# Second half of q and k of the first batch: from SP's queue with casts on chip to POOL's queue, cast on the way in

## The chip, the cores and the metric

The kernel runs on one core of one Trainium2 chip. The metric is the device time of one execution in microseconds (us), lower is better. Each kernel was executed several times; executions of two kernels are compared only where they ran in the same rounds on the same chip.

The profiles name the engines in short: PE is TensorE's matmuls (PEld its loading of weights), DVE is VectorE, ACT is ScalarE, POOL is GpSimd, SP is SyncE, which here only issues DMA transfers. "Clock" is the share of full speed that the profile shows as granted to TensorE.

## The reference

Symmetric sliding-window attention (8 batches, 8 heads, 576 positions, head size 64, window 32 to each side), then a two-layer network with an ELU over 4608 tokens:

```python
def _attn_ref(q, k, v):
    scores = scale * np.matmul(q, k.transpose(0, 1, 3, 2))
    mask = np.abs(pos[:, None] - pos[None, :]) <= 32
    scores = np.where(mask, scores, -1e9)
    attn = softmax(scores)                      # cut
    return np.matmul(attn, v)

def _moe_ref(x, w_in, w_out):                   # w_in 512x2048, w_out 2048x512
    h = x @ w_in
    g = np.where(h > 0.0, h, np.exp(np.minimum(h, 0.0)) - 1.0)
    return g @ w_out
```

Inputs and output are f32. The kernel computes in bf16 with f32 accumulation.

## The kernel before

Tokens go in 18 tiles of 256. A tile's hidden layer takes 8 steps (`mm1`), and so does its output layer (`mm2`); attention blocks are worked in pairs of 64 queries, two pairs to a tile. The first two tiles are interleaved: four hidden steps of the first, four of the second. A first step needs the pairs of its tile, so the start of the kernel is a race of loads: q and k (two halves of the first batch), values, and quarters of the weights.

```python
def load_qk(b, which, part, engs=(nc.sync, nc.sync)):       # f32 into SBUF, SP's queue
    ...
    for h in range(2):
        engs[h].dma_start(out=t[:, h, :], in_=src[:, :, h, :])

def load_v(b, m):                                           # f32 -> bf16 on the way, POOL's queue
    nc.gpsimd.dma_start(out=V_e[b % 3][p0:p1, m, :, 0:D], in_=...)

for which in range(2):
    load_qk(0, which, HALF_A, (nc.sync, nc.scalar))
...
for m in (1, 0, 2):
    load_v(0, m)
# ... masks ...
gate(masks[0:1, 3, 0:1])            # a 1-element DMA on SP: holds SP's queue until masks are done
for which in range(2):
    load_qk(0, which, HALF_B)       # four SP loads of 288 KB
load_w_in(0)                        # POOL's queue from here
for m in (3, 4):
    load_v(0, m)
load_w_out(0); load_w_in(1); load_w_out(1)
...
def transpose_qk(b, which, part, j0, n, evac, tag="t0"):
    for j in range(n):
        nc.tensor.transpose(pt[:, j * 128:(j + 1) * 128], src[:, j0 + j, :], ident)
    ...                              # eviction to qT or kT
...
# pairs 0 and 1, then hidden step 0 and 1, then:
front_cast(0, HALF_B, nc.scalar)     # f32 -> bf16 on ACT
front_cast(1, HALF_B, nc.vector)     # and on DVE
at(1, "mid", front_transpose, 1, HALF_B, nc.scalar, ("s", "u"))
at(1, "mid", front_transpose, 0, HALF_B, nc.vector, ("y0", "y1"))
for i, tag in ((2, "s"), (3, "u")):
    at(1, "mid", scores, i, tag)
    at(1, "mid", exponential, i)
    at(2, "dve", mask, i)
```

`idle(n, tag)` puts n matmuls on zeros into PE's program ("fillers"), to keep its clock up. `at(kk, slot, ...)` places work beside hidden step kk.

The softmax here doesn't subtract the row's maximum and nothing guards it: scores larger than these inputs give would overflow.

## Time and profile before

| | before |
|---|---|
| first three timed runs | 314.39, 320.15, 315.09 us |
| profiled run, its span | 310.77 us, 309.1 us |
| PE busy, of it in the first 30 us | 292.7 us, 22.3 us |
| second half of k landed | 17.4 us |
| hidden step 2 starts, first hidden step of tile 2 starts | 24.68, 27.98 us |

I call the last entry **the mark**. It is the first matmul of hidden step 4, and PE is nearly full from there on.

A line of VectorE's (DVE's) order of time, in the profile of the kernel before, shows the wait that the change is aimed at (start, length, instruction, then idle time before it and what ended it):

```profile
17.43 0.83 DVE L234 CAST qkb<-f 128x640 bf16<-128x640 f32 x2 [3.23 <-DMA f<-in_k_dram]
```

DVE sat idle for 3.23 us until k was there, and transposes, evictions and scores come behind it.

### The profile page before, as it was taken

What the parts mean: (1) busy time and instruction counts of PE and PEld (TensorE: products, weight loads), DVE (VectorE), ACT (ScalarE), POOL (GpSimd) and SP (SyncE); (2) the same over time, 40 slices, a digit from 0 to 9 for tenths busy, and PEclk for the clock granted to TensorE, in tenths of its full rate; (3) what the DMA queues carried; (4) which work ended last, traced back from release to release, by engine and by line L of the source; (5) the groups of instructions that cost most, each with busy time, mean ns of one, the idle gap of its engine ahead of it and who ended that gap; (6) DMA issues with size and microseconds to landing.
All of it is one profiled execution on the core that took longest, in us unless ns stands there. A gap on an engine that the chain in (4) does not pass through costs nothing.

```text
span 309.1 us, 7510 instructions
## 1 busy us (share of the span) xinstructions
PE 292.7 (95%) x2996; PEld 197.8 (64%) x3048; DVE 247.0 (80%) x480; ACT 170.6 (55%) x256; POOL 43.8 (14%) x60
## 2 busy tenths in 40 slices
PE   7768999999999999999999999999999999999994
PEld 3446666676666666666766666666666666666662
DVE  6677788899979788888888888888888787876663
ACT  3564756687664674667366736673636363634331
POOL 8733000834101112020202010000000000000000
PEclk9999999999999999999999999999999999999999
DMA  9999999999999999999989999488111111111011
GB/s 191 225 202 233 230 204 383 338 190 241 298 160 180 247 240 196 220 185 317 266 164 143 209 306 193 126 164 171 70 36 68 36 70 35 70 34 70 0 70 69
DMA packets 91657, 52.93 MB, mean 171 GB/s; under 512 B 76518, under 2 KB 80614, under 8 KB 91622
## 3 DMA queue, kind: packets, MB, share of 16 engines
q1 hardware_dynamic: 48022, 36.77, 46.7%
q0 software_dynamic: 41728, 8.92, 37.4%
q10 hardware_dynamic: 1872, 6.75, 6.7%
q8 instruction: 24, 0.39, 0.6%
q14 instruction: 11, 0.09, 0.1%
HBM read 36.70 MB, written 15.34 MB: 168 GB/s over the span
## 4 chain that ended last, share of the span: by engine, by line
PE 82%; DVE 7%; issue 3%; DMA 3%; ACT 2%; POOL 2%; SPq 1%; DVEq 0%; POOLq 0%
PE ps L558 38%; PE psY L592 36%; PE psS L320 3%; PE psS L288 3%; DMA f<-in_k_dram 3%; DVE g_sb L577 2%; DVE pm L308 1%; PE ptx L271 1%; DVE m_sb L567 1%; POOL Ve L129 1%; ACT e_sb L565 1%; DVE x_st L332 1%; ACT pu L299 1%; DVE y_sb L234 1%; SPq L123 1%
## 5 line engine op out<-in xcount | busy, mean ns | idle before, releaser
L565 ACT ACTIVATE e_sb<-ps 128x512 f32<-128x512 f32 (+1 forms) x145 | 86.2, 594 | 119.6 <-PE ps L558 112.8
L558 PE MATMUL ps<-xT,w_in_sb 128*128 128x256 bf16 x1152 | 149.3, 273 | 1.9 <-ACT xT L232 1.2
L592 PE MATMUL psY<-w_out_sb,g_sb 128*128 128x512 bf16 x525 | 139.1, 379 | 3.1 <-issue 0.6
L558 PEld LDWEIGHTS <-w_in_sb 128*128 128x128 bf16 x1152 | 110.7, 98 | 40.4 <-issue 2.2
L577 DVE SCALAR_TENSOR_TENSOR g_sb<-ps,m_sb 128x512 bf16<-128x512 f32 (+1 forms) x145 | 99.5, 686 | 12.9 <-PE ps L558 0.5
L567 DVE TENSOR_SCALAR m_sb<-e_sb 128x512 bf16<-128x512 f32 (+1 forms) x145 | 62.3, 430 | 33.0 <-ACT e_sb L565 30.8
L592 PEld LDWEIGHTS <-g_sb 128*128 128x128 bf16 x576 | 54.5, 98 | 38.3 <-DVE g_sb L577 0.2
L129 POOL DMA_DIRECT2D Ve<-in_v_dram x40 | 34.6, 876 | 131.7 <-PE psS L320 92.5
L299 ACT ACTIVATE pu<-psS 128x1024 bf16<-128x1024 f32 x36 | 36.5, 1020 | 3.5 <-PE psS L288 3.5
L232 ACT CAST qkb<-f 128x768 bf16<-128x768 f32 (+3 forms) x32 | 26.7, 838 | 0.0
L308 DVE TENSOR_TENSOR pm<-pu,masks 128x1024 bf16<-128x1024 bf16 x36 | 24.6, 683 | 1.9 <-ACT pu L299 1.8
L332 DVE TENSOR_TENSOR x_st<-psS,rc 128x512 bf16<-128x512 f32 x36 | 24.9, 692 | 1.2
L320 PEld LDWEIGHTS <-pm 128*64 128x64 bf16 x576 | 11.2, 110 | 10.5 <-DVE pm L308 7.4
L320 PE MATMUL psS<-Ve,pm 128*64 128x65 bf16 x320 | 13.7, 196 | 0.9 <-DVE pm L308 0.8
L140 DVE COPY Vo<-Ve 64x1040 bf16<-64x1040 bf16 x32 | 13.7, 428 | 1.0
L288 PE MATMUL psS<-qT,kT 64*128 64x64 bf16 x576 | 12.2, 193 | 2.4 <-DVE qT L234 1.9
L288 PEld LDWEIGHTS <-kT 64*128 64x128 bf16 x576 | 9.9, 96 | 7.0 <-issue 5.2
L234 DVE COPY y_sb<-psY 128x512 f32<-128x512 f32 x18 | 12.3, 686 | 1.1 <-PE psY L592 0.9
L320 PE MATMUL psS<-Vo,pm 128*64 128x65 bf16 x256 | 12.5, 197 | 0.2 <-DVE pm L308 0.2
L234 DVE CAST qkb<-f 128x1152 bf16<-128x1152 f32 (+3 forms) x14 | 9.2, 679 | 4.0 <-DMA f<-in_k_dram 3.6
L232 ACT COPY y_sb<-psY 128x512 f32<-128x512 f32 x18 | 10.5, 583 | 2.2 <-PE psY L592 2.2
L271 PE MATMUL ptx<-ident,qkb 128*128 128x128 bf16 x108 | 8.9, 235 | 1.7 <-DVE qkb L234 1.7
(32 smaller groups left out, 67.3 us busy)
## 6 DMA issues: line engine op xcount, KB each, us to landing
out_dram<-y_sb SPq DMA_DIRECT2D x35, 256.0 KB, 2.5
f<-in_q_dram SPq DMA_DIRECT2D x12, 576.0 KB, 9.0
f<-in_k_dram SPq DMA_DIRECT2D x12, 576.0 KB, 10.4
in_dram<-qkb ACTq DMA_DIRECT2D x10, 576.0 KB, 8.4
Ve<-in_v_dram POOLq DMA_DIRECT2D x24, 128.0 KB, 11.0
w_in_sb<-in_moe_w_in_dram POOLq DMA_DIRECT2D x4, 512.0 KB, 16.2
w_out_sb<-in_moe_w_out_dram POOLq DMA_DIRECT2D x4, 512.0 KB, 17.1
f<-in_q_dram SPq DMA_DIRECT2D x7, 288.0 KB, 6.3
```

What stands on the lines that cost most here:

```text
L129: nc.gpsimd.dma_start(out=V_e[b % 3][p0:p1, m, :, 0:D], in_=v[b, :, lo + p0:lo + p1, :].rearrange("h p d -> p h d"))
L232: nc.scalar.copy(d_, s_)
L288: nc.tensor.matmul(psS[:, h % 2, hp * 128 + z * QB:hp * 128 + (z + 1) * QB], lhsT=kT[b % 2][base:base + 64, KPAD + hp * S + QB * qb - WIN: ...
L299: nc.scalar.activation(pu, _bap(psS, [psS.ap[0], [1, 1024]]), AX.Exp, scale=SCALE)
L308: nc.vector.tensor_mul(pm, pu, _bap(mm, [mm.ap[0], [0, H], [1, 2 * QB]]))
L320: nc.tensor.matmul(psS[QB * z:QB * (z + 1), par, hp * VD:(hp + 1) * VD], lhsT=pm[:, par * HP + hp, z * QB:(z + 1) * QB], rhs=vv[:, qb // 2 ...
L332: nc.vector.tensor_mul(x_st, _bap(psS, [psS.ap[0], [VD, HP], [512, 2], [1, D]]), _bap(rc, [rc.ap[0], [2, HP], [1, 2], [0, D]]))
L558: nc.tensor.matmul(ps[:, j, :], lhsT=w_in_sb[:, do, fo * 128:(fo + 1) * 128], rhs=xT[t][:, :, do, :], start=(do == 0), stop=(do == NDO - 1))
L565: nc.scalar.activation(e_sb, ps, AX.Exp)
L567: nc.vector.tensor_scalar(m_sb, e_sb, -1.0, None, ALU.add)
L577: nc.vector.scalar_tensor_tensor(g_t[kk][:, z * w:(z + 1) * w, :], ps, 0.0, m_t[kk][z], ALU.max, ALU.min)
L592: nc.tensor.matmul(psY[t][ts], lhsT=g_sb[:, j, ts * 128:(ts + 1) * 128], rhs=w_out_sb[:, s * FG + j, :], start=(s == 0 and j == 0), stop=( ...
```

## The change

Its intent: get the second half of q and k out of SP's queue, where it competes with POOL's weights; put it in POOL's own queue at the place where it is wanted; let the DMA cast it; and so have it early enough to transpose between the first value products and score pairs 2 and 3 between hidden steps 0 and 1. Since a cast DMA lays the two heads of a couple out apart, each 128x128 transpose becomes a couple of 128x64 ones. Cut to its core:

```diff
+    def load_cast(b, which, part):
+        t = cpool.tile([128, 2, nj * D], BF16, name=f"c{which}")
+        ...
+        for h in range(2):
+            nc.gpsimd.dma_start(out=t[:, h, :], in_=src[:, :, h, :])
...
-    gate(masks[0:1, 3, 0:1])
-    for which in range(2):
-        load_qk(0, which, HALF_B)
-    load_w_in(0)
-    for m in (3, 4):
-        load_v(0, m)
-    load_w_out(0)
-    ...
+    for which in range(2):
+        load_cast(0, which, HALF_B)
+    load_w_in(0)
+    # two mask selects and a third
+    load_w_out(0)
+    for m in (3, 4):
+        load_v(0, m)
+    ...
+    gate(w_out_sb[0:1, NFO // 4 - 1, D_MODEL - 1:D_MODEL])   # was: w_in_at(1)
+    for which in range(2):
+        load_qk(1, which, HALF_A)
...
+                for h in range(2):
+                    nc.tensor.transpose(
+                        pt[64 * h:64 * (h + 1), j * 128:(j + 1) * 128],
+                        qk_c[b, which, z][:, h, (j0 + j) * D:(j0 + j + 1) * D], ident)
...
     pv(0)
-    idle(2, "h0")
+    front_transpose(0, HALF_B, nc.scalar, ("h0", "h1"))
     pv(1)
...
+    front_transpose(1, HALF_B, nc.vector, ("y0", "y1"))
     x_transpose(1)
-    front_cast(0, HALF_B, nc.scalar)
-    front_cast(1, HALF_B, nc.vector)
...
+    at(0, "mid", scores, 2, "s")
+    at(0, "mid", exponential, 2)
+    at(0, "mid", scores, 3, "u")
+    at(1, "mid", exponential, 3)
...
-            at(kq - 1 + which, "mid", cast_qk, 1, which, part, 0, SJ // 2,
+            at(*((kq + which, "dve") if kq == 7 else (kq - 1 + which, "mid")),
+               cast_qk, 1, which, part, 0, SJ // 2,
...
-        for n in {1: (0,), 2: (), 3: ()}.get(
+        for n in {1: (0,), 2: (), 3: (), 4: (), 5: (2,), 6: (3, 4)}.get(
```

More of the change, by code (lines that the diff above doesn't have):

```diff
@@ L123, in load_qk @@
             engs[h].dma_start(out=t[:, h, :], in_=src[:, :, h, :])
+    qk_c = {}
+    def load_cast(b, which, part):
+        z, nj = part
+        t = cpool.tile([128, 2, nj * D], BF16, name=f"c{which}")
+        qk_c[b, which, z] = t
+        src = (q, k)[which][b, :, z * NC * nj:(z + 1) * NC * nj, :].rearrange(
+            "(g h) (c j) d -> c g h (j d)", h=2, j=nj)
+        for h in range(2):
+            nc.gpsimd.dma_start(out=t[:, h, :], in_=src[:, :, h, :])
     def load_v(b, m):
@@ L183, in edges @@
                 nc.vector.memset(_bap(z, [z.ap[0], [S, n], [1, WIN]]), 0.0)
+    ident = cpool.tile([128, 128], BF16)
+    make_identity(nc, ident)
     edges(0)
     edges(1)
-    ident = cpool.tile([128, 128], BF16)
-    make_identity(nc, ident)
     masks = cpool.tile([128, 5, QB], BF16, name="masks")
@@ L202 @@
         load_v(0, m)
-    for mi in (0, 4):
-        nc.gpsimd.affine_select(
-            out=masks[:, mi, :], in_=masks[:, mi, :], compare_op=ALU.is_ge,
-            fill=0.0, base=-WIN, pattern=[[0, QB]], channel_multiplier=1)
-    nc.gpsimd.affine_select(
-        out=masks[:, 3, :], in_=masks[:, 3, :], compare_op=ALU.is_ge,
-        fill=0.0, base=128 - WIN - 1, pattern=[[0, QB]],
-        channel_multiplier=-1)
-    kinds = ["FE", "EE", "EL", "LF"]
-    gate(masks[0:1, 3, 0:1])
-    for which in range(2):
-        load_qk(0, which, HALF_B)
-    load_w_in(0)
-    for m in (3, 4):
-        load_v(0, m)
-    load_w_out(0)
-    load_w_in(1)
-    load_w_out(1)
+    kinds = ["FE", "EE", "EL", "LF"]
     def kind(jb):
@@ L264, in transpose_rows, with transpose_qk, evict @@
             out=keys_or_queries(b, which), in_=in_dram.pop((b, which)))
-    def transpose_qk(b, which, part, j0, n, evac, tag="t0"):
+    def transpose_qk(b, which, part, j0, n, evac, tag="t0", later=None):
         z, nj = part
-        src = qk_b[b, which, z]
         pt = ps_tile([128, 1024 if n <= 8 else 2048], BF16, tag, "ptx")
         for j in range(n):
-            nc.tensor.transpose(
-                pt[:, j * 128:(j + 1) * 128], src[:, j0 + j, :], ident)
-        d = keys_or_queries(b, which)
-        copy_on(evac,
-                _bap(d, [d.ap[0], [S, HP], [nj, NC], [1, n]],
-                     z * NC * nj + j0),
-                _bap(pt, [pt.ap[0], [1, HP], [HP, NC], [128, n]]))
+            if (b, which, z) in qk_c:
+                for h in range(2):
+                    nc.tensor.transpose(
+                        pt[64 * h:64 * (h + 1), j * 128:(j + 1) * 128],
+                        qk_c[b, which, z][:, h, (j0 + j) * D:
+                                          (j0 + j + 1) * D], ident)
+            else:
+                nc.tensor.transpose(
+                    pt[:, j * 128:(j + 1) * 128],
+                    qk_b[b, which, z][:, j0 + j, :], ident)
+        def evict():
+            d = keys_or_queries(b, which)
+            copy_on(evac,
+                    _bap(d, [d.ap[0], [S, HP], [nj, NC], [1, n]],
+                         z * NC * nj + j0),
+                    _bap(pt, [pt.ap[0], [1, HP], [HP, NC], [128, n]]))
+        if later is None:
+            evict()
+        else:
+            later.append(evict)
     st = {}
@@ L369, in front_cast, with front_transpose @@
             cast_qk(0, which, part, j0, n, eng)
-    def front_transpose(which, part, evac, tags):
+    def front_transpose(which, part, evac, tags, later=None):
         for (j0, n), tag in zip(SPLIT, tags):
-            transpose_qk(0, which, part, j0, n, evac, tag)
+            transpose_qk(0, which, part, j0, n, evac, tag, later)
     def idle(n, tag):
@@ L383 @@
     nc.scalar.activation(warm, zeros[:, 0:1], AX.Exp)
+    for which in range(2):
+        load_cast(0, which, HALF_B)
+    load_w_in(0)
+    for mi in (0, 4):
+        nc.gpsimd.affine_select(
+            out=masks[:, mi, :], in_=masks[:, mi, :], compare_op=ALU.is_ge,
+            fill=0.0, base=-WIN, pattern=[[0, QB]], channel_multiplier=1)
+    nc.gpsimd.affine_select(
+        out=masks[:, 3, :], in_=masks[:, 3, :], compare_op=ALU.is_ge,
+        fill=0.0, base=128 - WIN - 1, pattern=[[0, QB]],
+        channel_multiplier=-1)
+    load_w_out(0)
+    for m in (3, 4):
+        load_v(0, m)
+    for c in (1, 2):
+        load_w_in(c)
+        load_w_out(c)
+    for m in range(3):
+        load_v(1, m)
+    load_w_in(3)
+    load_w_out(3)
+    for m in range(3, VS):
+        load_v(1, m)
+    gate(w_out_sb[0:1, NFO // 4 - 1, D_MODEL - 1:D_MODEL])
+    for which in range(2):
+        load_qk(1, which, HALF_A)
+    gate(w_in_at(3))
+    for which in range(2):
+        load_qk(1, which, HALF_B)
+    for which in range(2):
+        load_qk(2, which, WHOLE)
     idle(8, "y1")
@@ L404 @@
         normalize(i)
-    for i in (0, 1):
-        idle(1, "h1")
-        x_transpose(i)
-        x_evac(i, nc.scalar)
-    idle(2, "h1")
-    front_cast(0, HALF_B, nc.scalar)
-    front_cast(1, HALF_B, nc.vector)
-    load_w_in(2)
-    load_w_out(2)
-    for m in range(3):
-        load_v(1, m)
-    load_w_in(3)
-    load_w_out(3)
-    for m in range(3, VS):
-        load_v(1, m)
-    gate(w_in_at(1))
-    for which in range(2):
-        load_qk(1, which, HALF_A)
-    gate(w_in_at(3))
-    for which in range(2):
-        load_qk(1, which, HALF_B)
-    for which in range(2):
-        load_qk(2, which, WHOLE)
+    x_transpose(0)
+    x_evac(0, nc.scalar)
+    front_transpose(1, HALF_B, nc.vector, ("y0", "y1"))
+    x_transpose(1)
+    x_evac(1, nc.scalar)
+    idle(2, "h1")
     tasks = {}
@@ L449, in pair_at @@
         at(kk + 2, "end", x_evac, i, nc.scalar)
-    at(1, "mid", front_transpose, 1, HALF_B, nc.scalar, ("s", "u"))
-    at(1, "mid", front_transpose, 0, HALF_B, nc.vector, ("y0", "y1"))
-    at(2, "dve", rotate_v, 0, 2, VS - 1)
-    for i, tag in ((2, "s"), (3, "u")):
-        at(1, "mid", scores, i, tag)
-        at(1, "mid", exponential, i)
-        at(2, "dve", mask, i)
-    at(2, "dve", lambda: mm2(1))
+    at(0, "mid", scores, 2, "s")
+    at(0, "mid", exponential, 2)
+    at(0, "mid", scores, 3, "u")
+    at(1, "mid", exponential, 3)
+    at(1, "dve", mask, 2)
+    at(2, "dve", lambda: mm2(1))
+    at(2, "dve", rotate_v, 0, 2, VS - 1)
+    at(2, "dve", mask, 3)
     for i in (2, 3):
@@ L472 @@
                nc.scalar, "s")
-    at(8, "dve", edges, 2)
+    at(6, "dve", edges, 2)
     at(16, "dve", hold_v, 2)
```

## The prediction

> **What bounds the kernel now.** I read the page first: the busy row, the slices, the chain. The span is 309.1 us (profiled run 310.77, median of the unprofiled runs 315.09).
>
> ```profile
> PE 292.7 (95%) x2996; PEld 197.8 (64%) x3048; DVE 247.0 (80%) x480; ACT 170.6 (55%) x256; POOL 43.8 (14%) x60
> ```
>
> TensorE is the bound, so only a stretch in which PE waits can give time. The table of busy times by stretch says where that is (columns: stretch, its length, busy us of PE, PEld, DVE, ACT, POOL, then granted clock, DMA share, GB/s).
>
> ```profile
> 10.00:15.00 5.00, 4.11 (x58) 1.92 (x52) 3.04 (x7) 2.69 (x4) 3.40 (x5) 1.00 1.20 275
> 15.00:20.00 5.00, 3.22 (x35) 2.56 (x34) 2.46 (x6) 3.95 (x7) 0.74 (x2) 1.00 1.52 209
> 20.00:25.00 5.00, 3.57 (x74) 2.19 (x75) 4.62 (x9) 1.94 (x2) 2.48 (x4) 1.00 1.24 206
> 25.00:30.00 5.00, 4.01 (x37) 3.23 (x37) 3.59 (x8) 2.74 (x5) 1.43 (x3) 1.00 1.22 228
> 30.00:35.00 5.00, 5.00 (x42) 3.44 (x41) 3.15 (x7) 2.90 (x5) 0.53 (x1) 1.00 1.58 266
> ```
>
> With the two earlier rows (3.59 and 3.76) PE is busy 22.26 of the first 30 us, and 20 of those matmuls are fillers on zeros. From 30 us on it is nearly full. So the change acts on a start-up of 30 us, and what it is worth is how much sooner PE reaches the full stretch. The mark I use is the first hidden-layer matmul of the second token tile, at 27.98. PE in order of time, around the hole:
>
> ```profile
> 15.32 1.91 PE L558 MATMUL ps<-xT,w_in_sb 128*128 128x256 bf16 x16 [0.24 <-ACT xT L232]
> 17.98 1.24 PE L271 MATMUL ptx<-ident,qkb 128*128 128x128 bf16 x18 [0.75 <-DVE qkb L234]
> 21.14 0.64 PE L288 MATMUL psS<-qT,kT 64*128 64x64 bf16 x32 [1.92 <-DVE qT L234]
> 21.80 1.90 PE L592 MATMUL psY<-w_out_sb,g_sb 128*128 128x512 bf16 x7
> 24.68 1.05 PE L558 MATMUL ps<-xT,w_in_sb 128*128 128x256 bf16 x8
> 27.98 1.03 PE L558 MATMUL ps<-xT,w_in_sb 128*128 128x256 bf16 x8 [0.94 <-ACT xT L232]
> ```
>
> And the chain of waits of the same stretch (start, length, what):
>
> ```profile
> 6.17 0.21 POOL masks L207
> 6.38 0.02 issue
> 6.39 0.75 SPq L151
> ...
> 9.29 8.12 DMA f<-in_k_dram
> 17.40 0.02 issue
> 17.43 0.83 DVE qkb L234 x2
> ...
> 19.73 1.36 DVE qT L234 x2
> 21.09 0.04 issue
> 21.14 0.42 PE psS L288 x16
> ```
>
> The second half of q and k sits behind a gate on the masks (6.39), is issued by SP from 7.20 to 9.9 and lands at 14.0 to 17.4. Then come casts (17.43), transposes (17.98), evictions to 21.09 and the scores of pairs 2 and 3. But the weights arrive hardly sooner. The list of DMA issues (KB, us to landing), for issues between 9.7 and 10.5 with the one before still running:
>
> ```profile
> w_out_sb<-in_moe_w_out_dram POOLq DMA_DIRECT2D x1, 512.0 KB, 12.9
> w_in_sb<-in_moe_w_in_dram POOLq DMA_DIRECT2D x1, 512.0 KB, 14.5
> ```
>
> The first quarter of w_out, issued at 8.88, lands at 21.8, and the first matmul on it starts at 21.80. The second quarter of w_in, issued at 9.80, lands at 24.3; its first use is at 24.68. So there are two bounds within half a microsecond: the q/k chain and POOL's queue. **Removing the q/k chain alone would gain next to nothing; the question is what the same bytes do to POOL's queue.**
>
> **What the Trainium skill says.** "DMA: Bandwidth & Descriptors", Rules for kernel authors, has casts during a DMA issued from GpSimd. The trace agrees: values and weights go from f32 in HBM into bf16 tiles that way, and queue 0 counts 8.92 MB over the run, half of the 17.8 MB of f32 read. The same page, Issuing engines are not separate DMA queues, says all issuers share the same 16 DMA engines. The trace agrees: from 12 to 14 us SP's queue took 0.58 MB and POOL's only 0.05 MB. "TensorE: Matmul & The Clock Gate", Part 3, says small matmuls on different column groups run at once. The trace agrees: 32 matmuls of the 128*64 form go in couples with the same start, 16 couples in 0.45 us, 28 ns a couple. Part 1 of that page puts the array at half rate after an idle window of about 3.4 us; here the first eight fillers take 0.45 us each and later ones about 0.21, and no later PE wait exceeds 1.92 us.
>
> **The change, part by part.**
>
> *Removed.* The gate and four SP loads of 288 KB; ACT casts at 15.16 (1.25 us), DVE casts at 17.43 (0.83); four fillers at about 0.21 us. All this lies in a stretch where PE waits, so only the end of the chain counts.
>
> *Added on POOL.* Four issues. Rows for w_in, w_out cost 0.76 to 0.94 each, so 4 x 0.76 = 3.0 us: 5.4 to 8.4 instead of nothing. w_in's first quarter is then issued at 8.4, not 6.33. The mask selects (1.0 us) end near 10.3; the first mask multiplication was at 10.97, so still in time.
>
> *Transfers.* In the trace POOL's queue moves 205 GB/s counted in bf16 on weights (0.82 MB from 20 to 24 us) and 153 on values (6 to 8 us). The first three values are through at 8.45. Behind them, with no other queue running:
> - q half, 2 x 147 KB: 1.44 us, to 9.9; k half, to 11.3.
> - w_in quarter 0, 524 KB: 2.56 us, to 13.85; w_out quarter 0: to 16.4.
> - two values, 246 KB at 153: 1.6 us, to 18.0; w_in quarter 1: to 20.6.
>
> A semaphore comes later than the bytes: adding up the moved bytes, w_out 0 was through at 19.7 and landed at 21.8, w_in 1 at 22.3 and 24.3; for the early values it was about 1.1. I choose 2.0 for all but values late in the queue (2.6). So q lands near 11.9, k 13.3, w_in 0 15.9, w_out 0 18.4, values 20.6, w_in 1 22.6. The new gate on w_out 0 lets the next batch's loads go near 19; at the old gates SP's bytes began 3 to 4.5 us after the issue, so w_in 1 is through before they compete.
>
> *PE up to the first hidden layer.* The first value product was at 11.7 to 12.1. The q transposes follow at once: 9 couples at about 55 ns, 0.5 us (the old 9 transposes took 0.50 to 0.58; a couple streams the same 128 columns). Second value product, transpose of x, then 0.5 us of k transposes near 13.6, second x transpose near 14.3, where it was 14.25. ACT's two evictions (0.75 + 0.62) fit after the exponentials end at 11.79 and before x at 13.85; DVE's k evictions (1.4 us) end near 15.7. The first hidden matmul then waits for w_in 0: **15.9, 0.6 later than the 15.32 of before.**
>
> *From there.* Hidden step 0 to 16.8; scores 2 and 3 (0.64) to 17.4; step 1 to 18.3. ACT takes 0.60 + 1.02 + 0.60 + 1.02 from 16.9; DVE 0.42 + 0.69 + 0.69 + 0.42 + 0.69, to about 20.4. Output step 0 starts at 18.5 (w_out there at 18.4), step 1 at 20.4. The values of 20.6 are rotated (0.88, to 21.5), the mask of pair 3 ends at 22.2, its value product at 22.65. Hidden step 2 starts then, w_in 1 being there at 22.6: 22.65 against 24.68. The same four steps as before follow (3.3 us), so the mark falls to 25.95 from 27.98. **Sum: +0.6 at the first hidden step, -2.6 behind it, 2.0 us gained.** The output steps put off to loop steps 5 and 6 keep w_out 1 (through near 26, landed near 27.5) off PE, with hidden step 5 in its place. After that PE is full and the 2 us go to the end undiminished.
>
> **Rivals.**
> 1. *POOL's queue stays the bound and gives nothing.* If cast rows of 2,304 B run at the 153 of the values, everything behind comes 1 us later; if the early SP loads take their share sooner, w_in 1 or w_out 1 is late by up to 3 us. For it: SP's 0.58 against 0.05 MB. Against it: total bytes per quarter do not grow, and the trough near 9 us (20 to 100 GB/s) goes. Time: 314 to 316.
> 2. *The landing lag is smaller without competition.* With the 1.1 of the early values the arrivals allow a gain of 3 us, but ACT and DVE then bind, through exponentials and masks. Time: 312 to 312.5.
> 3. *PE becomes the bound at the transposes or runs cold.* If couples do not overlap, 36 transposes add 1 us; with four fillers gone, a long wait for w_in 0 might halve the rate. Only transposes, products and two fillers remain from 12 to 15 us. Against: no gap over about 1 us is in sight. Time: 314 to 315.
> 4. *It is hidden anyway.* The casts' removal alone would be, by the w_out landing at 21.8. The reordering of w_out ahead of two values is what rescues it.
>
> **Range and chances.** 315.09 - 2.0 = 313.1. Rivals 1 and 3 pull to 315 or a little over, 2 to 312; fast runs differ by about 0.3%, 1 us, and an 0.8 us run spread is in the given times (314.39, 315.09). Range 310.9 to 315.4. Faster by over 2% needs 6.3 us, of the 7.7 idle in the first 30, which no step gives: 0.02. Slower by 6.3 us would take a hole of a kind that I do not see: 0.02.
>
> **What the after-profile shows if right.** The q half landing near 12 and k near 13.3; no q/k cast before the next batch; hidden steps 0 and 1 split by scores, at 15.5 to 16; step 2 near 22.6; the mark near 26; from 30 us the same full PE. Couples of transposes with the same start prove the 0.5 us. It is wrong if step 0 or 2 sits behind a weight landing later than I put it, if PE waits at the k transposes, or if PE, given the 2 us, loses them by 60 us through a wait for w_out 1 or for the next batch's casts.

## The result, and the profile after

The changed kernel took 309.59, 309.89, 310.10 and 309.13 us: **median 309.74**. The kernel before had a median of 314.74 us over four runs (the first three and one of 313.66 beside the changed kernel), or 314.39 over the three of them that are fast. The ratio is 0.985, interval 0.9816 to 0.9885; ratios here are the mean time of one kernel's fast runs over that of the other's in the same rounds, so not quite the ratio of the medians that I quote. Executions over 1.5% slower than the fastest of the same kernel are left out of the means. The predicted time was 313.1 and the range 310.9 to 315.4; the measured time lies below the range.

Later, both kernels ran on one chip in the same rounds: 313.02 against 309.73, ratio 0.9902 (0.986 to 0.9943). Later the kernel before was executed 44 times; the 43 fast ones took from 310.10 to 315.11, mean 312.85. Ten executions of the changed kernel have a mean of 309.87. So the gain is about **3 us, 1%**, and the first figure of 1.5% owes part of its size to the three earliest runs of the kernel before, whose median of 315.09 no later call reached. They were not traced, so what they lost is open.

PE in order of time in the changed kernel's profile, the lines that answer to the six of before (`ptx<-ident,c` are the couples of transposes; L582 is the hidden layer, L296 scores, L616 the output layer):

```profile
11.83 0.67 PE L266 MATMUL ptx<-ident,c 128*64 128x128 bf16 x18
13.57 0.69 PE L266 MATMUL ptx<-ident,c 128*64 128x128 bf16 x18
15.27 1.03 PE L582 MATMUL ps<-xT,w_in_sb 128*128 128x256 bf16 x8 [0.46 <-ACT xT L226]
16.23 0.64 PE L296 MATMUL psS<-qT,kT 64*128 64x64 bf16 x32
18.72 1.02 PE L616 MATMUL psY<-w_out_sb,g_sb 128*128 128x512 bf16 x3 [0.87 <-DMA w_out_sb<-in_moe_w_out_dram]
22.64 1.05 PE L582 MATMUL ps<-xT,w_in_sb 128*128 128x256 bf16 x8 [0.36 <-DMA w_in_sb<-in_moe_w_in_dram]
25.95 1.91 PE L582 MATMUL ps<-xT,w_in_sb 128*128 128x256 bf16 x16 [0.94 <-DVE m_sb L591]
```

Both transposes run without a wait, scores 2 and 3 start at 16.23 and not at 21.14, and the wait for q and k is gone. Hidden step 2 starts at 22.64 (before 24.68) and waits 0.36 us for w_in's second quarter. The mark is at 25.95, which is the very figure that I had predicted (to the hundredth by chance: in a second profile of the same kernel it is 26.09). POOL's part, in order of time:

```profile
5.38 1.12 POOL L135 DMA_DIRECT2D c<-in_q_dram  x2
6.46 1.32 POOL L135 DMA_DIRECT2D c<-in_k_dram  x2
7.75 0.78 POOL L167 DMA_DIRECT2D w_in_sb<-in_moe_w_in_dram  x1
```

The four issues take 2.4 us, and the first quarter of w_in goes out at 7.75 instead of 6.33. The chain of waits of this profile now has one long piece in the start-up:

```profile
11.50 11.10 DMA w_in_sb<-in_moe_w_in_dram
22.59 0.05 issue
22.64 1.06 PE ps L582 x8
```

That is POOL's queue delivering the second quarter of w_in: this queue now bounds the start-up, though only by the 0.36 us that PE waits for it at 22.64.

So the trace of the changed kernel came out as told, and still the time was missed by 3.4 us. Comparing the two profiles gives 310.77 - 309.59 = 1.2 us: 2.0 at the mark, of which 0.8 is lost behind it. The rest of the answer is in the kernel before: its first profile was of one of its quickest executions. The experiments are about that.

### The profile page after: what moved, and what is told of

Read it like the earlier page. It is cut to its first block, busy times and chain, and to the rows that moved or that the text cites. A ratio compares the mean times of both kernels' runs of the same rounds, so it can differ in the third digit from the quotient of the medians.

```text
span 307.9 us, 7525 instructions
## 1 busy us (share of the span) xinstructions
PE 291.5 (95%) x3009; PEld 196.9 (64%) x3062; DVE 245.8 (80%) x478; ACT 169.4 (55%) x254; POOL 45.8 (15%) x64
## 4 chain that ended last, share of the span: by engine, by line
PE 81%; DVE 7%; DMA 4%; POOL 3%; issue 2%; ACT 1%; DVEq 0%; POOLq 0%
PE ps L582 38%; PE psY L616 36%; DMA w_in_sb<-in_moe_w_in_dram 4%; PE psS L328 3%; PE psS L296 3%; DVE g_sb L601 2%; POOL Ve L141 1%; PE ptx L271 1%; DVE m_sb L591 1%; DVE x_st L340 1%; DVE pm L316 1%; ACT e_sb L589 1%; POOL c L135 1%; DVE y_sb L228 1%; PE psXT L349 1%
## 5 line engine op out<-in xcount | busy, mean ns | idle before, releaser
L582 PE MATMUL ps<-xT,w_in_sb 128*128 128x256 bf16 x1152 | 149.3, 273 | 2.7 <-DVE m_sb L591 0.9
L616 PE MATMUL psY<-w_out_sb,g_sb 128*128 128x512 bf16 x525 | 139.1, 379 | 4.2 <-DMA w_out_sb<-in_moe_w_out_dram 0.9
L582 PEld LDWEIGHTS <-w_in_sb 128*128 128x128 bf16 x1152 | 110.7, 98 | 41.0 <-issue 2.3
L616 PEld LDWEIGHTS <-g_sb 128*128 128x128 bf16 x576 | 54.5, 98 | 39.9 <-DVE g_sb L601 1.6
L226 ACT CAST qkb<-f 128x768 bf16<-128x768 f32 (+1 forms) x30 | 25.4, 848 | 0.0
L296 PEld LDWEIGHTS <-kT 64*128 64x128 bf16 x576 | 10.0, 97 | 5.3 <-issue 4.2
L296 PE MATMUL psS<-qT,kT 64*128 64x64 bf16 x576 | 12.4, 193 | 0.5 <-DVE kT L228 0.5
L226 ACT COPY qT<-ptx 128x1152 bf16<-128x1152 bf16 (+2 forms) x8 | 7.5, 971 | 3.1 <-PE ptx L271 2.4
L271 PE MATMUL ptx<-ident,qkb 128*128 128x128 bf16 x90 | 7.1, 223 | 2.0 <-DVE qkb L228 1.9
```

What stands on the lines that cost most here:

```text
L226: nc.scalar.copy(d_, s_)
L296: nc.tensor.matmul(psS[:, h % 2, hp * 128 + z * QB:hp * 128 + (z + 1) * QB], lhsT=kT[b % 2][base:base + 64, KPAD + hp * S + QB * qb - WIN: ...
L582: nc.tensor.matmul(ps[:, j, :], lhsT=w_in_sb[:, do, fo * 128:(fo + 1) * 128], rhs=xT[t][:, :, do, :], start=(do == 0), stop=(do == NDO - 1))
L616: nc.tensor.matmul(psY[t][ts], lhsT=g_sb[:, j, ts * 128:(ts + 1) * 128], rhs=w_out_sb[:, s * FG + j, :], start=(s == 0 and j == 0), stop=( ...
```

## The experiments

The theories at the start: **A**, in the kernel before, the SP loads and POOL's loads compete, and k lands sometimes much later than in the first profile; **B**, the array clock falls back in the hole behind the wait for k; **C**, only another chip. Behind all of them stands the prediction's account of the changed kernel, part by part.

### The kernel before again: e0_before_again, h1_before_look, h2_before_look, h3_before_look

No edit. Four more executions were profiled.

> The kernel before, unchanged. Its profiled run took 310.77 us, its timed runs 313.66 to 320.15, while the changed kernel took 309.13 to 310.10 everywhere. Theory A (the old start-up has a wait that comes and goes, because the SP loads of q and k and POOL's loads of weights compete for the 16 DMA engines): times spread over 3 us or more, from about 310.5 to 315, and if the profile falls in a long run it shows a weight or q/k landing later than in the first profile by the amount lost. Theory B (the array clock is granted late or falls back in some runs of the old kernel): the long runs list a granted clock below that of the short ones, with the landings where they were. Theory C (nothing but another chip): all runs of the kernel before on this chip lie within 1 us of each other and the ratio of this copy to it is 1.000.

> The kernel before, one more profile. Theory A (landing of k): a run of 312.5 to 315 has k landing at 18.5 to 20.5, its mark (first hidden step of the second tile) moved by the same, and 282.5 to 283.5 us behind the mark. Theory B (clock): k near 17.5, a clock of 0.5 to 0.6 for some 3 us before the mark. Neither: mark near 28 and more than 284 us behind it.

> As the one before it, another execution: the same three readings. If theory A holds in both, mark minus k landing stays at 10.6 to 11.7 without a clock fall-back, and is about 1.4 more with one.

> As the two before it, a third execution. Over the three: if the times differ by over 1 us, the landings of k should differ by about the same (theory A), or the clock should have fallen back in the longer ones alone (theory B).

The copy e0 took 311.94 (310.11 to 313.16) beside 312.54 (311.07 to 315.11), ratio 0.9966 (0.9927 to 1.0004). So C is out as it stood: on one chip, one kernel spreads over 4 us, and its copy differs by 0.3% with five rounds. DVE's line for the cast that waits for k, in e0, then in h1:

```profile
17.74 0.83 DVE L234 CAST qkb<-f 128x640 bf16<-128x640 f32 x2 [4.03 <-DMA f<-in_k_dram]
```

```profile
18.63 0.83 DVE L234 CAST qkb<-f 128x640 bf16<-128x640 f32 x2 [4.57 <-DMA f<-in_k_dram]
```

k came 0.3 us later in e0 and 1.2 later in h1. And busy times by stretch (its length, then PE, PEld, DVE, ACT, POOL, then the granted clock, DMA share, GB/s), first the first profile of before, then e0:

```profile
18.00:20.00 2.00, 1.21 (x18) 1.07 (x19) 1.89 (x5) 1.37 (x2) 0.56 (x1) 1.00 1.31 205
20.00:22.00 2.00, 0.84 (x33) 0.63 (x33) 1.97 (x4) 0.42 (x1) 1.19 (x2) 1.00 1.24 205
22.00:24.00 2.00, 1.95 (x23) 0.92 (x22) 1.68 (x4) 1.52 (x2) 0.84 (x1) 1.00 1.24 206
24.00:26.00 2.00, 1.78 (x36) 1.55 (x31) 1.86 (x5) 0.24 (x1) 0.74 (x1) 1.00 1.24 206
```

```profile
18.00:20.00 2.00, 1.24 (x18) 1.01 (x18) 1.89 (x6) 1.22 (x2) 1.31 (x2) 1.00 1.24 205
20.00:22.00 2.00, 0.55 (x32) 0.61 (x32) 1.97 (x4) 0.24 (x2) 1.27 (x2) 1.00 1.25 207
22.00:24.00 2.00, 2.00 (x13) 0.77 (x7) 1.67 (x4) 1.84 (x2) 0.34 (x1) 0.58 1.24 206
24.00:26.00 2.00, 2.00 (x36) 0.89 (x34) 0.58 (x2) 0.00 (x0) 0.40 (x1) 0.57 1.24 207
```

In the column of the clock, e0 has 0.58 and 0.57 from 22 to 26 us, where the first profile has 1.00. The instructions show it too: output steps 0 and 1, with the value products of pair 2 or 3 not counted, stretch over 3.35 us from 22.03, against 1.90 from 21.80. All five profiles of the kernel before, unchanged:

| profile | cast of k starts | clock under 0.9 near 20 to 26 us | scores of pair 2 start | step 2 | mark | mark minus cast | mark minus scores | time | time minus mark |
|---|---|---|---|---|---|---|---|---|---|
| first | 17.43 | no | 21.14 | 24.68 | 27.98 | 10.55 | 6.84 | 310.77 | 282.8 |
| e0 | 17.74 | yes | 21.45 | 26.11 | 29.41 | 11.67 | 7.96 | 312.38 | 283.0 |
| h1 | 18.63 | yes | 22.70 | 27.38 | 30.69 | 12.06 | 7.99 | 313.68 | 283.0 |
| h2 | 17.95 | yes | 21.66 | 25.99 | 29.30 | 11.35 | 7.64 | 311.90 | 282.6 |
| h3 | 18.14 | yes | 21.84 | 26.18 | 29.48 | 11.34 | 7.64 | 312.05 | 282.6 |

The last column hardly moves, so all the difference between these executions arises ahead of the mark. **Both A and B hold.** The first profile is the one with the earliest k and the only one without a fall-back. The mean cast start is 17.98, so 0.55 later than in the first profile. From the cast to the scores all take 3.70 or 3.71 us except h1, which takes 4.07, as one DVE instruction there (L567) takes 0.79 us and not 0.42. From the scores to the mark the four with a fall-back take 0.80 to 1.15 us more than the first profile, 0.97 on average, 0.77 spread over five. Together with h1's 0.36 (0.07 over five) that is 1.39, and the mean mark of 29.37 is 1.39 behind the first one. (How the DMA engines share is told in "DMA: Bandwidth & Descriptors", Queues, rings and completion order: each engine goes round the queues that have work, packet by packet. The order of arrival here fits such sharing; which packet held up which is not shown for these five.)

In the hole, PE was not wholly idle. From the start of hidden step 0 to the scores, h2 (15.81 to 21.66) and the first profile (15.32 to 21.14) have the same pattern: 3.16 and 3.15 us busy, with waits of 0.77 and 1.92 in the one, 0.75 and 1.92 in the other. Yet h2's clock fell, at 21.1, and the first profile's did not. "TensorE: Matmul & The Clock Gate", Part 1, has the activity window run free, of about 3.4 us; equal business with different outcome agrees with that, and so does the length of the fall-backs: each of the four lasts 3.4 us, in h2 from 21.1 to 24.5.

The executions that were not traced list a mean clock, and it goes with the time. Of the 43 fast ones, the eight with 0.997 or more took 310.10 to 311.62, mean 310.94; the other 35 took 311.07 to 315.11, mean 313.29. This does not say where in a run the clock fell, and not every fall costs time: h3 has another one from 7.6 to 11 us, and its hidden step 0 still starts at 15.21.

### Fillers in the hole: f1_before_fillers

```diff
+    at(1, "mid", idle, 4, "y0")
     at(1, "mid", front_transpose, 1, HALF_B, nc.scalar, ("s", "u"))
     at(1, "mid", front_transpose, 0, HALF_B, nc.vector, ("y0", "y1"))
+    at(1, "mid", idle, 5, "h0")
```

> The kernel before with nine more filler matmuls in the two idle stretches between hidden step 1 and the scores of pair 2 (17.0 to 18.0 and 19.2 to 21.1 in its profile), nothing else. In the second profile of the kernel before, the granted clock was 0.58 and 0.57 from 22 to 26 us, after PE had been busy 2.67 of the 6 us from 16 to 22, and hidden step 2 started at 26.11 instead of 24.68; in the first profile it stayed at 1.00 after 3.30 of 6 busy. Theory B (the array clock falls back behind this hole in most executions): no fall-back here, times near 310.5 to 311 and hardly spread, 1 to 2 us below the kernel before. Theory A (competition of transfers): the fillers change nothing, 312 to 313, spread as before.

It took 312.48 (310.79 to 313.22) beside 313.64 (310.10 to 314.33 without the slow one), ratio 0.9962 (0.9914 to 1.0009): a gain of 1.2 us in the medians that the interval does not secure. In the profile the clock stayed at 1.00 throughout the first 30 us, and all six executions list 0.997 or more, where ten of the eleven beside them list 0.995 or less. So fillers do keep the clock up. PE at the scores and at the mark:

```profile
23.18 0.64 PE L288 MATMUL psS<-qT,kT 64*128 64x64 bf16 x32 [0.91 <-DVE qT L234]
30.04 1.03 PE L560 MATMUL ps<-xT,w_in_sb 128*128 128x256 bf16 x8 [0.94 <-DVE m_sb L569]
```

Between the two lie 6.86 us, as in the first profile (6.84) and within 0.01 of e3, g1, f5 and h4, which have no fall there either, and unlike the four with a fall-back (7.64 to 7.99): the extra time there is the clock's. But k landed late, its cast at 19.02. Of the 2.06 us by which this mark is behind the first profile's, 1.59 is the late k and 0.45 lies between cast and scores, where again one DVE instruction was long (0.88 us). B by itself does not make the kernel as quick as its first profile, nor as the changed kernel. The expected 310.5 to 311 was a miss.

### The first quarter of w_out ahead of two values: e3_before_wout_first, f4_wout_first_fillers

```diff
     load_w_in(0)
+    load_w_out(0)
     for m in (3, 4):
         load_v(0, m)
-    load_w_out(0)
```

f4 has the fillers of f1 as well.

> The kernel before with only the first quarter of w_out put ahead of the last two values on POOL's queue. My prediction said that this reordering rescues the change; in the kernel before the q and k chain ends at 21.1 us in any case, so alone it should give at most 0.5 us if the profile of before is typical. If timed runs of before are long because w_out's first quarter lands late (theory A), it takes 2 to 4 us off, to 310.5 to 312. If theory B or C holds, it stays within 0.5 us of the kernel before.

> The earlier run with the first quarter of w_out ahead of the last two values (315.43, against 312.54 of the kernel before) with the same nine fillers. Theory B: that run was long because the clock fell back twice, so with the fillers it comes to 311 to 312.5. Theory A (its two values land later and hold the value products up): it stays at 314 to 315.5.

e3 took 315.43, ratio 1.0082 (1.0044 to 1.012): slower by less than 2%, but clear of the noise, where I had expected nothing or a gain. f4 took 313.89, ratio 1.0019 (0.9974 to 1.0065). In the profiles k's cast started at 18.86 (e3, the quickest of its six runs at 312.75) and at 20.83 (f4, 315.58). DVE's line in f4:

```profile
20.83 1.20 DVE L234 CAST qkb<-f 128x640 bf16<-128x640 f32 x2 [6.63 <-DMA f<-in_k_dram]
```

DVE waited 6.63 us for k, and PE's clock was at 0.50 from 20.4 to 27.3 us, in and behind so large a hole, nine fillers or not. So moving POOL's loads about, with SP's loads untouched, changes when SP's loads land: that is the competition of theory A, and the way in which the kernel before was exposed to it. The counts of packets show it. From 14 to 16 us, SP's queue moved 257 packets with 0.51 MB in the first profile, and POOL's 628 small ones of values with 0.08 MB. With w_out's larger packets in the place of the values, it was 187 packets with 0.38 MB against 191 with 0.19 MB in f4, and 189 with 0.40 MB against 189 with 0.19 MB in e3. From 16 to 18 us SP's queue had 0.02 MB left to move in the first profile, 0.29 in f4 and 0.40 in e3. (e3's profile lost more than that: its first half of k was late as well, with its cast at 8.56 where before had 6.44, the clock was at 0.50 from 9.0 to 15.8, and hidden step 0 started at 18.28. That load was issued before anything which e3 changed, so this part is chance.)

### SP's loads without the gate: g1_no_gate

```diff
-    gate(masks[0:1, 3, 0:1])
     for which in range(2):
         load_qk(0, which, HALF_B)
```

> The kernel before without the gate on the masks: the four SP loads of q and k's second half go out at 2.1 us instead of 7.2, ahead of POOL's values and weights. In five profiles of the kernel before and its variants the last of them landed at 17.4, 17.7, 18.9, 19.0 and 20.8 us, and the time of the run followed: 310.77, 312.38, 312.75, 312.59, 315.58. If this landing is what makes the kernel before long and uneven (theory A): it lands by 12 us, the casts no longer wait, the rest is bound by w_in's second quarter (24.3 before), and the time is 310 to 311.5 with a spread under 1.5 us, though the first value products start 1 to 2 us later. If the clock is the cause (theory B), or what is left after these is the same, 312 to 314.

It took 313.29 (312.67 to 314.63), ratio 1.001 (0.997 to 1.0051): no gain. k no longer keeps anything waiting (its casts start at 16.95, in turn and with no wait), but DVE's and PE's lines show what came in its place:

```profile
12.68 0.43 DVE L140 COPY Vo<-Ve 64x1040 bf16<-64x1040 bf16 x1 [2.24 <-DMA Ve<-in_v_dram]
```

```profile
18.16 1.91 PE L557 MATMUL ps<-xT,w_in_sb 128*128 128x256 bf16 x16 [0.24 <-ACT xT L231]
```

The values are late now: their copy starts at 12.68 where before had 9.08, hidden step 0 at 18.16 instead of 15.32, and the mark at 29.68. The first half of k was late too (its cast at 7.82, before 6.44). Early or late, the same bytes of q and k in a second queue cost the first pairs or the second ones. I had expected 310 to 311.5 from the landing of k alone; its place relative to the values counts as much. With the two starts tried for SP's loads (behind the masks, and at once) it did not come between the first three values and the weights; in POOL's queue the program puts it just there. A gate on the values themselves, with SP's queue kept, was not tried.

### The transport alone, and its place in the queue: f5_loads_only, h4_loads_behind_w_in

f5 is the changed kernel with PE's order of before: transposes after hidden step 1, then scores 2 and 3, and the four fillers back.

```diff
     pv(0)
-    front_transpose(0, HALF_B, nc.scalar, ("h0", "h1"))
+    idle(2, "h0")
     pv(1)
...
-    front_transpose(1, HALF_B, nc.vector, ("y0", "y1"))
...
-    at(0, "mid", scores, 2, "s")
...
+    at(1, "mid", front_transpose, 1, HALF_B, nc.scalar, ("s", "u"))
+    at(1, "mid", front_transpose, 0, HALF_B, nc.vector, ("y0", "y1"))
+    for i, tag in ((2, "s"), (3, "u")):
+        at(1, "mid", scores, i, tag)
```

h4 is f5 with the cast loads behind the first quarter of w_in:

```diff
+    load_w_in(0)
     for which in range(2):
         load_cast(0, which, HALF_B)
-    load_w_in(0)
```

> The transport part of the change alone: cast loads of q and k on POOL's queue, no casts on chip, couples, new gate and output places, but PE's order of before, the transposes after hidden step 1 and scores 2 and 3 behind them. If the landings set the gain (my prediction's account: w_in's second quarter at 22.6), hidden step 2 starts at 22.6 to 23.2 and the time is within 0.5 us of the changed kernel, 309.5 to 310.5. If the order is what fills the hole and keeps the clock up (theory B), PE idles some 2 us while the evictions run near 19, and part of the executions are 1.5 us longer: median 310.5 to 312.

> The earlier run with the transport part alone (310.61), with the four cast loads of q and k behind the first quarter of w_in instead of ahead of it, still in POOL's queue. If one queue instead of two is what counts: q and k land near 15 to 16.5 in every execution, hidden step 0 starts at 15.0 to 15.5 instead of 16.2, and the time is 309.8 to 310.8 with a spread under 1.5 us. If the place ahead of the weights counts: the landings come after hidden step 1 is done, PE waits for them, 311.5 to 313.

f5 took 310.61 (310.13 to 311.21), ratio 0.9915 (0.9873 to 0.9958), so the transport brings most of the gain or all of it; its new queue and the removal of the casts on chip come together in it and were not tried apart. Its profile has the mark at 27.74, 1.8 behind that of the changed kernel; one piece of that is hidden step 0, at 16.20 behind a 0.91 us wait for w_in, and there is no fall-back. h4 took 310.73 (309.58 to 312.06), ratio 0.9964 (0.9917 to 1.0012). Its profiled run, the quickest of six at 309.58, has step 0 at 14.77, no wait for q and k, and the mark at 26.29. Its slower runs are not traced, and the interval includes no gain at all. So the two places in the queue, and what the new order of PE's work adds to the transport, are not told apart by these times (0.9902, 0.9915 and 0.9964, with intervals that overlap).

### Parts of the change undone: e1_late_gate, e2_old_outputs, g2_values_first

e1 puts the next batch's loads back behind the second quarter of w_in, e2 the output steps back to their old places, g2 the first quarter of w_out behind the two values.

```diff
-    gate(w_out_sb[0:1, NFO // 4 - 1, D_MODEL - 1:D_MODEL])      # e1
+    gate(w_in_at(1))
...
-        for n in {1: (0,), 2: (), 3: (), 4: (), 5: (2,), 6: (3, 4)}.get(      # e2
+        for n in {1: (0,), 2: (), 3: ()}.get(
...
-    load_w_out(0)                                                # g2
     for m in (3, 4):
         load_v(0, m)
+    load_w_out(0)
```

> The changed kernel with the old place of the next batch's loads: they wait for the second quarter of w_in (landed 22.6) instead of the first quarter of w_out (18.7). If the earlier loads of batch 1 are part of the gain (theory A's competition, in reverse), this is 1 to 3 us slower than the changed kernel, with the casts of batch 1 waiting. If they are a side matter (the early landing of q and k does it all), 309.5 to 310.5, as the changed kernel.

> The changed kernel with the output steps in their old places (step 2 after hidden step 4, not after 5). w_out's second quarter landed at 26.8 in the changed kernel's profile and hidden step 4 ended there near 26.8: if putting the outputs off is needed, PE waits 0.5 to 2 us at 26.8 and the time is 310 to 312; if not, it is 309 to 309.8, a little better, because the two output steps no longer stand together.

> The changed kernel with the first quarter of w_out behind the last two values, as in the kernel before. My prediction said that the reordering rescues the change. If so: w_out lands near 20.3 instead of 18.7, PE idles 2.4 us before output step 0, hidden step 2 starts near 23.0 to 23.5 and the time is 0.4 to 2 us above the changed kernel (the upper end if the clock falls back in this hole). If the second quarter of w_in is the bound whatever the order of what comes before it: within 0.3 us of the changed kernel.

e1 took 310.00, ratio 0.9907 (0.9874 to 0.994), and e2 310.23, ratio 0.9914 (0.9881 to 0.9946), the changed kernel 0.9902: neither part is needed for the gain. Their marks are at 25.85 and 26.19. g2 took 310.44 (308.97 to 312.76), ratio 0.9912 (0.986 to 0.9963). What this order risks is in its profile. PE, and then busy times by stretch:

```profile
20.45 2.64 PE L616 MATMUL psY<-w_out_sb,g_sb 128*128 128x512 bf16 x7 [2.40 <-DMA w_out_sb<-in_moe_w_out_dram]
```

```profile
18.00:20.00 2.00, 0.05 (x1) 0.10 (x1) 1.90 (x4) 1.55 (x3) 1.20 (x2) 1.00 1.24 206
20.00:22.00 2.00, 1.50 (x5) 0.64 (x6) 1.67 (x4) 0.00 (x0) 0.75 (x1) 0.86 1.24 205
22.00:24.00 2.00, 2.00 (x35) 1.11 (x33) 0.22 (x2) 0.00 (x0) 0.74 (x1) 0.50 1.24 206
```

PE idled for 2.40 us, the hole that I had worked out for this order. The clock then fell to 0.50, and the mark came at 27.73 against 26.09 in the changed kernel's profile of this call. Other executions of g2 took 308.97 and 309.01 with listed clocks of 1.000 and 0.998, so the fall-back is hardly there in all. A hole in the changed kernel brings the fall-back, as in the kernel before; with w_out ahead of the values the hole is 0.87 us (0.54 in the second profile), and neither of the two profiles of the changed kernel has a fall-back between 16 and 30 us.

### The changed kernel again and a candidate: g3_after_again, f2_after_casts_back, g4_candidate_again

g3 has no edit. f2 and g4 are one and the same kernel:

```diff
     at(1, "mid", exponential, 3)
+    at(1, "mid", idle, 3, "y0")
+    at(4, "dve", idle, 3, "s")
...
-            at(*((kq + which, "dve") if kq == 7 else (kq - 1 + which, "mid")),
+            at(kq - 1 + which, "mid",
                cast_qk, 1, which, part, 0, SJ // 2,
```

> The changed kernel itself, for a direct comparison on this chip. 309.1 to 310.3, spread 1 to 1.5 us, mark (first hidden step of the second tile) at 25.8 to 26.2.

> A candidate beyond the changed kernel: the casts of batch 1's first half back in their old places (loop steps 6 and 7), and three fillers each in the two holes that are left (near 17.9 and 25.0). In the changed kernel's profile PE waited 0.41 us for the k cast at 35.24, and 0.8 of the 2.0 us gained by 25.95 was gone by 38. If those slots are the cause, it takes 0.3 to 0.6 us off: 309.2 to 309.6 where the changed kernel would be near 309.9. If PE there is short of other things (evictions, output steps in a row), it equals it.

> The candidate of before (casts of batch 1 in their old places, six more fillers), beside the changed kernel on one chip. Its profiled run took 308.57 with the mark at 25.90, so 282.7 us behind the mark where the changed kernel takes 283.6. If this is real: 0.4 to 0.9 us below the changed kernel. If it was chance: equal.

g3 took 309.73 (309.16 to 311.49) and g4 309.18 (308.81 to 309.78), ratios to the kernel before 0.9902 and 0.9876 (0.9839 to 0.9913); f2 had 309.39, ratio 0.9872 (0.9827 to 0.9916). The candidate beats the kernel before, and in the medians the changed kernel by 0.55 us. The intervals overlap, so this last step is likely and not secured. What it removes is in PE's order of time, the k transposes of the next batch, in the changed kernel's first profile and in g4:

```profile
35.24 0.68 PE L271 MATMUL ptx<-ident,qkb 128*128 128x128 bf16 x9 [0.41 <-DVE qkb L228]
```

```profile
34.90 0.67 PE L271 MATMUL ptx<-ident,qkb 128*128 128x128 bf16 x9
```

The wait of 0.41 us for the cast of k is gone. Time behind the mark is 283.6 in the changed kernel's first profile, 283.0 in g4 and 282.7 in f2; it is 283.1 to 283.6 in the five other variants that have the new slots of the casts (e1, e2, f5, h4, g2), and 282.6 to 283.0 in the five profiles of the kernel before, which has the old ones.

The profiled run of g3 was the longest of its six, 311.49, with the mark at 26.09 as ever. It lost its time much later. PE's waits in it, over 30 to 312 us (what waited, for what: total us, times, longest):

```profile
PE ps L582 <- DVE g_sb L601: 1.6, 2, 1.0
PE psS L296 <- DMA kT<-in_dram: 0.7, 1, 0.7
```

The same table of the changed kernel's first profile has one wait of 0.6 in the first line and nothing in the second. PE was busy 9.08 of the 10 us from 100 to 110 and 8.88 of those from 120 to 130, where the first profile has 9.79 and 9.89. So the changed kernel has another source of long runs, a later batch whose transposed keys come late. It is in one of two profiles; how often it comes is not known, and no experiment was made on it.

## Why the prediction was wrong

- **The changed kernel's course: right, in part by errors that cancel.** q landed at 10.4 and 11 (foreseen 11.9), k at 11.8 and 12.5 (13.3), w_in's first quarter at 15.05 (15.9), w_out's at 18.7 (18.4), the two values near 20.2 (20.6), w_in's second quarter at 22.6 (22.6). The four issues took 2.4 us and not 3.0. The two-us lag that I chose was too long early in the queue and right late in it. Hidden step 0 began at 15.27 and not at 15.9, step 2 at 22.64 (22.65), the mark at 25.95 (25.95). The couples took 0.56 us from their start to the next instruction's for q and 0.62 for k, against 0.5 foreseen. (One line was misread: the 32 matmuls with 16 couples in 0.45 us are the scores, of the 64*128 form; those of the 128*64 form, the value products, go in eight couples, which start within 0.25 us.)
- **The step that failed** is "no later PE wait exceeds 1.92 us", by which I set the clock aside, and what it stood on: I took the one trace of the kernel before for all its executions. In h2 and h3 the longest wait of that hole is 1.92 us as well, and the clock fell. "So the mark falls to 25.95 from 27.98" has the right first number and the wrong second one. In five traced executions the mark was at 29.37 on average, 0.55 of it from a later k and 0.77 from the clock. The prediction named the fall-back as a danger to the changed kernel (rival 3) and did not see that the kernel before was the one under it. At the mark the gain is 29.37 - 26.02 = 3.35 (the mean of two profiles of the changed kernel), not 2.03.
- **"Removing the q/k chain alone would gain next to nothing"** rested on the same trace: with k at 17.4, w_in at 24.3 was but 0.4 us from binding. With k at 17.7 to 18.6 and a fall-back, step 2 starts at 26.0 to 27.4, well behind that landing.
- **The base** was wrong as well, and by more: I subtracted a difference of traces from 315.09, though the trace belonged to a run of 310.77, and 43 later fast runs have a mean of 312.85, which is 2.2 us less. Of the miss of 3.2 us (313.1 against the mean of 309.87) these 2.2 are the base and 1.3 the gain at the mark; 0.8 lost behind the mark goes the other way, and 0.5 is not assigned. Subtracted from the traced run, 2.0 would have given 308.8, less than the measured time. From the mean of the five traced runs, 312.16, minus 3.35, plus the 0.8, comes 309.6. Why the untraced runs are 0.7 longer than the traced ones on average is not shown.
- **"After that PE is full and the 2 us go to the end undiminished": wrong by 0.8 us** in the first profile. The candidate's time behind the mark, back at that of the kernel before, points to the casts' new slots; by its times alone that is likely and not secured.
- **The rivals.** 1 (POOL's queue stays the bound) is right as to the bound, as the 11.10 us piece in the chain shows, and wrong as to the gain. 2 (smaller landing lag) held for the early landings and gained nothing at the mark. 3 did not come for the changed kernel between 16 and 30 us: the early clock dip in its profile (0.75 from 5 to 10 us) did not move step 0, which was at 15.19 in e1 without a dip. 4 said that the order of w_out rescues the change: with the old order the gain is still there (0.9912), with an execution in it that shows the fall-back.
- The range was too narrow on the low side, because it held nothing for the spread of the kernel before: I put fast runs within about 0.3%, and the 43 later ones lie within 1.6%. The sign was there, in 314.39 to 320.15 beside a profile of 310.77. (The "0.8" between 314.39 and 315.09 is 0.7.)

Open: why the first three runs of the kernel before took 314 to 320 us, when 43 later fast ones had a mean of 312.85; what its executions over 313.7 contain, as none was traced (ten of these 13 list clocks of 0.988 or less, below any traced one); why SP's loads land at 17.4 in one execution and at 18.6 in another of the same kernel; and which part of the transport matters, the queue or the casts taken off the chip's engines.

## What to carry to other kernels

Before a difference of traces is subtracted from a median, compare the traced run with the timed ones: if they differ by more than the effect, trace the kernel several times and look for the landing and the clock that vary. A load that must come between two others can be put in their queue, at its place; in a second queue it came early here at the cost of one neighbour (g1), or late at the hands of the other (f4). A wait on TensorE can cost more than itself through the clock: behind waits of 1.92 to 2.29 us the fall-back cost 0.80 to 1.15 us more in four of five executions, so a change that closes such a hole may gain more than the wait.

## What the Trainium skill lacked or had wrong

- "TensorE: Matmul & The Clock Gate" (the table of goals at its end) advises against PE-idle gaps of more than about 3 us. Here the clock fell to half behind a gap of 2.40 us (g2), with PE fully in hidden step 1 before it and in output step 0 behind it. In the kernel before it fell with single gaps of 1.92 us (h2, h3), though there transposes stand between two gaps, and no run shows how they count. The page gives no share of busy time at which the clock falls.
- "DMA: Bandwidth & Descriptors" has fixed and variable costs of a transfer, but nothing on how far its landing moves from one execution to the next when two queues share the engines: the last of four SP loads of 288 KB landed from 17.4 to 18.6 us in five executions of one kernel, at 19.0 with nothing but PE fillers added, and at 20.8 in a variant with POOL's loads in another order.
- The same page has SWDGE at about 2.0 us plus bytes over 436 GB/s. Cast loads of 144 KB took 4.9 to 5.3 us from issue to landing, queued behind three value loads, and weights of 512 KB 7.3 us and more; a steady stream of them moved 205 GB/s counted in bf16. The page has no figure for a cast.
